# Splitting FFN weights: the last three bits as a byte in the sign word, the shift as an operation of its own

## The chip, the cores and the metric

The kernel runs on one core of one Trainium2 chip. The metric is the device time of one execution in microseconds, as the median of several runs. Lower is better.

## The reference

Attention with 32 global tokens and a local window, then a layer norm and a feed-forward block (FFN), all in float32. Cut to what matters:

```python
# q_l,k_l,v_l: (8, 8, 512, 64)   q_g,k_g,v_g: (8, 8, 32, 64)
out_g = softmax(scale * q_g @ k_all.T) @ v_all            # 32 global rows
s_ll  = where(|i - j| <= 32, scale * q_l @ k_l.T, -1e9)   # local band
out_l = softmax([scale * q_l @ k_g.T, s_ll]) @ [v_g, v_l]
x  = concat([out_g, out_l])       # (8, 576, 512) after heads are joined
xn = (x - mean(x)) / sqrt(var(x) + 1e-6) * g_ln
out = x + relu(xn @ w_ch1) @ w_ch2      # 512 -> 2048 -> 512
```

The two weight matrices, `w_ch1` (512 x 2048) and `w_ch2` (2048 x 512), come in as 64-bit floats.

## The kernel before, in words

**Chunks.** The 8 x 2 half sequences of local tokens are taken two at a time: eight chunks of 512 tokens, and a last chunk of the 256 global tokens. While TensorE does the FFN of one chunk, the attention of the next one runs beside it. The FFN loops over 16 blocks `f` of 128 hidden units. For each block TensorE makes `ph` (line 739: 12 matmuls, because each float is split into a high and a low part and three of the four products are kept), ScalarE writes its rectified high part `hh` (line 750), VectorE the low part `hl` (line 754), and TensorE adds 3 matmuls for each of four token tiles into `acc` (line 766).

**Weights.** A block of both matrices (128 partitions x 1024 elements) is loaded once as 64-bit words (`raw`, line 178) and turned into a high and a low 32-bit part that stay in on-chip memory for all chunks. The class `Weights` does that in steps, each one instruction on 128x1024 elements:

| step, token | line | engine | what it does |
|---|---|---|---|
| load, `wr` | 178 | SP queue | DMA of 1 MB into `raw` |
| head, `wa` | 183 | ScalarE | absolute value of the word with sign, exponent and high mantissa, scaled as a float to move the exponent, into `tmp` |
| tail, `wb` | 188 | ScalarE | makes the last three mantissa bits (0 to 7) from the upper half of the low word |
| bound, `wc` | 191 | VectorE | limits `tmp` to the largest float |
| join, `wd` | 195 | VectorE | shifts `tmp` left by 3 and ORs the three bits in |
| sign, `wg` | 201 | VectorE | ORs the sign in |
| high, `wh` | 208 | ScalarE | rounds to the high part `w[:, 0]` |
| low, `wl` | 212 | VectorE | `w[:, 1] = tmp - high` |

`tmp` has two buffers, so head of a block waits for low of the block two before it. All 16 blocks are split during the first chunk, between 17 and 125 us of the span.

**Order.** Every engine works in the order in which the program is written (`manual_schedule` covers all five). In the first chunk that order is the list of tokens `FIRST` (lines 50 to 71). Other tokens that matter here: `S`/`PS` scores on TensorE (lines 304, 428), `Rd`/`PRd` the reduction over scores on VectorE (321, 446), `Re`/`PRe` exponentials on ScalarE (335, 461), `C`/`PC` copies of turned probabilities (357, 481), `Na` the normalisation on VectorE (253), `Kt` transposes of normalised tokens on TensorE (667), `Kh` and `Kl` their high part on ScalarE (684) and low part on VectorE (688), `M`, `H`, `L`, `O` the four FFN steps of a block (739, 750, 754, 766), `X`/`PX` the attention output on VectorE (383, 519). A part of the list around joins 3 and 4:

```python
Kh1.0 wa4 Kl1.0 Kt1.1 wg3 PT0.1 Kh1.1 wb4 Kl1.1 wc4 Kt1.2 PC0.1 wd4 Kh1.2 Kt1.3 PV0 wh3
Kl1.2 Kh1.3 wl3 pv1 wr13 Kl1.3 wa5 wr14 PX0 Mb0 wr15 wb5 wg4 Mb1 Hb0 wc5 wh4 Lb0 PS1 wd5 Hb1
```

From the second chunk on the order comes from generators that hand out attention steps between the FFN's matmuls; among them are VectorE's 32x32 transposes (line 490) that the attention's second matmul (line 500) waits for.

Of the kernel before, what the change touches and what calls it, by code (L numbers as in the profile page):

```python
# [13 lines left out]
I32 = mybir.dt.int32  # L14
I16 = mybir.dt.int16
U16 = mybir.dt.uint16
BF16 = mybir.dt.bfloat16
I64 = mybir.dt.int64
AF = mybir.ActivationFunctionType
ALU = mybir.AluOpType  # L20
# [55 lines left out]

REBIAS = 2.0 ** -112
HUGE = 122877.9921875 * REBIAS
SIGN = -0x80000000


THIRD = 7.4999 / 65535

@with_exitstack
def attention_ffn_kernel(
# [11 lines left out]
    nc = tc.nc  # L97
# [71 lines left out]
    class Weights:  # L169
# [14 lines left out]

        def tail(self):
            third = self.raw.bitcast(U16).rearrange("p (n t) -> p n t", t=4)[:, :, 1]
            self.last = self.raw.bitcast(I32).rearrange("p (n t) -> p n t", t=2)[:, :, 0]
            nc.scalar.activation(self.last, third, AF.Copy, scale=THIRD)

        def bound(self):  # L190
            nc.vector.tensor_scalar(self.tmp, self.tmp, HUGE, None, ALU.min)

        def join(self):
            itmp = self.tmp.bitcast(I32)
            nc.vector.scalar_tensor_tensor(  # L195
                itmp, itmp, 3, self.last, ALU.logical_shift_left, ALU.bitwise_or
            )

        def sign(self):
            itmp = self.tmp.bitcast(I32)  # L200
            nc.vector.scalar_tensor_tensor(
                itmp, self.top, SIGN, itmp, ALU.bitwise_and, ALU.bitwise_or
            )

        def high(self):
# [910 lines left out]
```

## Time and profile before

| what | value |
|---|---|
| median of 3 runs | 937.46 us (937.17 to 938.05) |
| the profiled execution | 938.44 us, its span 936.7 us |
| mean granted TensorE clock in it | 0.989 |
| instructions | 21033 |

The span runs from the first to the last instruction of the profiled execution; the rest of that execution's time lies around it. The page gives busy time by engine, the span cut into 40 slices with busy tenths, the chain of work that ended last, and groups of instructions. Other views list waits (who waited for whom: total us, times, longest), the instructions of one tile (shortest, median and longest duration in ns, first and last start in us), a timeline (start, duration, engine, line; in brackets the idle time before it and what ended it), and busy time by stretch.

### The profile page before, as it was taken

The numbers are of one execution on the slowest core, as the hardware profiler recorded it, in microseconds if no ns is written. First come the engines' busy times: TensorE is split into PE (matmuls) and PEld (weight loads), VectorE is DVE, ScalarE is ACT, GpSimd is POOL, SyncE is SP. The second block draws the span as 40 slices with busy tenths as digits, with TensorE's granted clock in tenths as the row PEclk, the third lists the DMA queues.
The fourth block names the chain that finished last, engine by engine and source line by source line (L and its number), as shares of the span: only waits on it lengthen the run. The fifth ranks groups of instructions, "written<-read, shape, count | busy, mean of one in ns | idle before, by whom it ended". The sixth has DMA issues, their size and how long they took to land.

```text
span 936.7 us, 21033 instructions
## 1 busy us (share of the span) xinstructions
PE 911.1 (97%) x8652; PEld 722.4 (77%) x8652; DVE 572.0 (61%) x1852; ACT 313.4 (33%) x839; POOL 36.2 (4%) x121
## 2 busy tenths in 40 slices
PE   5899999999999999999999999999999999999997
PEld 3677777777778778777878778777877777777896
DVE  4999958765786657765776657765776623111311
ACT  5888733331323323231323323231422312211210
POOL 3000000000000000000000000000000000000000
PEclk9799999999999999999999999999999999999999
DMA  9993245212633263212533263213533151031100
GB/s 349 419 415 118 87 136 194 101 58 89 228 121 98 76 214 117 84 51 103 214 121 97 76 233 99 89 53 119 190 121 98 46 170 57 1 102 60 51 18 23
DMA packets 48880, 119.33 MB, mean 127 GB/s; under 512 B 5008, under 2 KB 16272, under 8 KB 45712
## 3 DMA queue, kind: packets, MB, share of 16 engines
q1 hardware_dynamic: 48784, 117.98, 35.4%
q8 instruction: 68, 1.11, 0.5%
q14 instruction: 28, 0.23, 0.1%
HBM read 100.14 MB, written 17.83 MB: 126 GB/s over the span
## 4 chain that ended last, share of the span: by engine, by line
PE 90%; DVE 2%; ACT 1%; issue 0%; DVEq 0%
PE acc L766 40%; PE ph L739 40%; PE sc L428 3%; PE pv L500 3%; PE t L667 1%; PE pv L620 1%; PE sc L566 1%; PE t L607 1%; DVE pt L490 1%; DVE w L212 0%; DVE tmp L195 0%; DVE ob L799 0%; ACT tmp L183 0%; ACT w L208 0%; DVE hl L754 0%
## 5 line engine op out<-in xcount | busy, mean ns | idle before, releaser
L766 PE MATMUL acc<-w,hh 128*128 128x512 f32 x1088 | 342.1, 396 | 0.0
L739 PE MATMUL ph<-xh,w 128*128 128x512 f32 (+1 forms) x1240 | 310.6, 377 | 0.2 <-DVE x L519 0.2
L754 DVE SCALAR_TENSOR_TENSOR hl<-ph,hh 128x512 fp32r<-128x512 f32 (+1 forms) x147 | 95.6, 651 | 279.0 <-ACT hh L750 278.6
L739 PEld LDWEIGHTS ph<-xh,w 128*128 128x128 f32 x1240 | 219.3, 189 | 47.4 <-issue 1.2
L750 ACT ACTIVATE hh<-ph 128x512 fp32r<-128x512 f32 (+1 forms) x147 | 83.1, 565 | 496.4 <-PE ph L739 496.3
L766 PEld LDWEIGHTS acc<-w,hh 128*128 128x128 f32 x1088 | 205.7, 189 | 45.7
L490 DVE STREAM_TRANSPOSE pt<-p 32x128 f32<-32x128 f32 x768 | 232.2, 302 | 11.1
L766 PE MATMUL acc<-w,hl 128*128 128x512 f32 x544 | 222.6, 409 | 0.3 <-DVE hl L754 0.2
L739 PE MATMUL ph<-xl,w 128*128 128x512 f32 (+1 forms) x524 | 143.8, 396 | 0.8 <-DVE xl L688 0.8
L766 PEld LDWEIGHTS acc<-w,hl 128*128 128x128 f32 x544 | 102.5, 188 | 26.5 <-issue 3.0
L739 PEld LDWEIGHTS ph<-xl,w 128*128 128x128 f32 x524 | 96.2, 189 | 26.2 <-issue 3.5
L461 ACT ACTIVATE p<-p,mn 128x128 f32<-128x128 f32 x224 | 87.2, 391 | 33.5 <-DVE mn L446 31.5
L446 DVE CUSTOM_DVE_ANT_0 p<-sc,mask 128x128 f32<-128x128 f32 x224 | 51.1, 285 | 0.1
L461 ACT ACTIVATION_READ_ACCUMULATOR p<-p,mn 128x1 f32 x224 | 42.0, 188 | 0.0
L500 PE MATMUL pv<-v,pt 128*32 128x64 f32 x1792 | 32.1, 222 | 2.3 <-DVE pt L490 2.3
L500 PEld LDWEIGHTS pv<-v,pt 128*32 128x32 f32 x1792 | 27.0, 111 | 8.9 <-issue 6.2
L428 PE MATMUL sc<-e 64*32 64x128 f32 x1792 | 32.4, 274 | 0.0
L428 PEld LDWEIGHTS sc<-e 64*32 64x32 f32 x1792 | 24.9, 105 | 9.5 <-issue 9.1
L242 ACT ACTIVATE x<-x,rs 128x512 f32<-128x512 f32 x30 | 22.8, 809 | 20.6 <-DVE rs L236 20.6
L688 DVE SCALAR_TENSOR_TENSOR xl<-t,g_sb,xh 128x512 fp32r<-128x512 f32 (+1 forms) x36 | 24.6, 689 | 7.9 <-ACT xh L684 7.7
L684 ACT ACTIVATE xh<-t,g_sb 128x512 fp32r<-128x512 f32 (+1 forms) x40 | 24.9, 624 | 12.0 <-PE t L667 11.8
L519 DVE TENSOR_TENSOR x<-pv,ri 128x256 f32<-128x256 f32 x56 | 21.2, 420 | 8.3 <-PE pv L500 5.7
(73 smaller groups left out, 477.0 us busy)
## 6 DMA issues: line engine op xcount, KB each, us to landing
v<-in_eu SPq DMA_DIRECT2D x28, 1024.0 KB, 7.1
e<-in_eu SPq DMA_DIRECT2D x28, 672.0 KB, 5.3
raw<-in_wd SPq DMA_DIRECT2D x16, 1024.0 KB, 12.7
gk<-in_gk SPq DMA_DIRECT2D x8, 1088.0 KB, 5.2
xs<-x SPq DMA_DIRECT2D x32, 256.0 KB, 7.1
ob<-xs SPq DMA_DIRECT2D x32, 256.0 KB, 7.3
out<-ob SPq DMA_DIRECT2D x32, 256.0 KB, 2.1
gv<-in_gv SPq DMA_DIRECT2D x16, 512.0 KB, 6.8
```

The source lines that it names most:

```text
L242: nc.scalar.activation(self.xn[:, j, :], self.x[:, j, :], AF.Identity, bias=self.rs[:, 1, j:j + 1], scale=self.rs[:, 0, j:j + 1],)
L428: nc.tensor.matmul(sc[h][gp, at:at + P], self.e[hd, j, w * WIN:(w + 1) * WIN], self.e[hd, j, k0 * WIN:(k0 + 4) * WIN], start=True, stop=Tr ...
L446: nc.vector.tensor_tensor_reduce(out=self.p[:, j, c], in0=self.sc[h][:, at:at + P], in1=masks[self.at[2], qb], scale=-QSCALE, scalar=BIG, ...
L461: nc.scalar.activation(self.p[:, j, c], self.p[:, j, c], AF.Exp, bias=self.mn[:, j, c:c + 1], scale=-1.0, accum_out=self.sm[:, j, c:c + 1],)
L490: nc.vector.transpose(out=self.pt[rp, j, :, gp], in_=self.p[gp, j, :, rp])
L500: nc.tensor.matmul(self.pv[gp, at:at + D], self.pt[:, j, 2 * h + qb, gp], self.v[:, j, 4 * qb + g, h * D:(h + 1) * D], start=True, stop=Tr ...
L684: nc.scalar.activation(hi, t[:, :n], AF.Copy, scale=g_sb[:, kt:kt + 1])
L688: nc.vector.scalar_tensor_tensor(lo, t[:, :n], g_sb[:, kt:kt + 1], f32(hi), ALU.mult, ALU.subtract)
L739: nc.tensor.matmul(ph[:, :n], w[:, kt, :], xx[kt][:, part.start:part.start + n], start=(i == 0), stop=(i == 3 * KT - 1),)
L750: nc.scalar.activation(hh[:, :n], self.ph[f, start][:, :n], AF.Relu)
L754: nc.vector.scalar_tensor_tensor(hl[:, :n], self.ph[f, start][:, :n], 0.0, f32(hh[:, :n]), ALU.max, ALU.subtract)
L766: nc.tensor.matmul(self.acc[t], a[:, ts], w, start=(f == 0 and i == 0), stop=(f == NF - 1 and i == 2),)
```

## The change

Tail writes its three bits no longer as a 32-bit number into the low word (whose content it had read), but as one byte into the lowest byte of the sign word, of which head has taken the absolute value before. Join then needs no second source: it is a shift by a constant, in place. Sign takes the sign bit and the three lowest bits of the sign word with one mask and ORs both in; it is still one instruction with two sources. The written order stays.

```diff
-SIGN = -0x80000000
+KEEP = -0x7FFFFFF9
...
         def tail(self):
             third = self.raw.bitcast(U16).rearrange("p (n t) -> p n t", t=4)[:, :, 1]
-            self.last = self.raw.bitcast(I32).rearrange("p (n t) -> p n t", t=2)[:, :, 0]
-            nc.scalar.activation(self.last, third, AF.Copy, scale=THIRD)
+            last = self.raw.bitcast(U8).rearrange("p (n t) -> p n t", t=8)[:, :, 4]
+            nc.scalar.activation(last, third, AF.Copy, scale=THIRD)
...
         def join(self):
             itmp = self.tmp.bitcast(I32)
-            nc.vector.scalar_tensor_tensor(
-                itmp, itmp, 3, self.last, ALU.logical_shift_left, ALU.bitwise_or
-            )
+            nc.vector.tensor_scalar(itmp, itmp, 3, None, ALU.logical_shift_left)
...
         def sign(self):
             itmp = self.tmp.bitcast(I32)
             nc.vector.scalar_tensor_tensor(
-                itmp, self.top, SIGN, itmp, ALU.bitwise_and, ALU.bitwise_or
+                itmp, self.top, KEEP, itmp, ALU.bitwise_and, ALU.bitwise_or
             )
```

More of the change, by code (lines that the diff above doesn't have):

```diff
@@ L16 @@
 U16 = mybir.dt.uint16
+U8 = mybir.dt.uint8
 BF16 = mybir.dt.bfloat16
```

## The prediction

> **What bounds the kernel now.** I read the page from the top: busy shares, the slices, then the chain that ended last.
>
> ```profile
> span 936.7 us, 21033 instructions
> PE 911.1 (97%) x8652; PEld 722.4 (77%) x8652; DVE 572.0 (61%) x1852; ACT 313.4 (33%) x839; POOL 36.2 (4%) x121
> PE   5899999999999999999999999999999999999997
> DVE  4999958765786657765776657765776623111311
> PE 90%; DVE 2%; ACT 1%; issue 0%; DVEq 0%
> ```
>
> TensorE (PE) is busy for 97% of the span and fills every slice after the first two or three (one slice is 23.4 us). VectorE (DVE) is full in slices 2 to 5, that is from about 23 to 117 us, where the weights are split. The change touches only that stretch, so the first question is where in it TensorE really waits. I asked for TensorE's waits from 58 us to the end:
>
> ```profile
> PE pv L500 <- DVE pt L490: 2.3, 3, 1.0
> PE ph L739 <- DVE x L519: 0.2, 1, 0.2
> ```
>
> Those are all: 0.2 us at the very start, and 2.3 us for the turned probabilities (L490), which come after the last weight. So from 58 us on nothing of the weight split holds TensorE up. A saving counts only if it brings TensorE's state at 58 us forward. The stretch before it, in columns PE, PEld, DVE, ACT, POOL, granted clock, DMA share and GB/s:
>
> ```profile
> 20.00:30.00 10.00, 6.12 (x168) 4.02 (x150) 8.16 (x40) 7.52 (x22) 0.82 (x2) 0.78 1.02 418
> 30.00:40.00 10.00, 7.81 (x89) 6.75 (x90) 9.58 (x20) 7.43 (x23) 1.59 (x4) 0.56 1.03 421
> 40.00:50.00 10.00, 9.62 (x142) 7.67 (x141) 9.83 (x32) 9.34 (x25) 1.29 (x3) 0.93 1.01 413
> 50.00:60.00 10.00, 8.03 (x111) 6.23 (x109) 9.78 (x16) 8.35 (x13) 0.35 (x1) 1.00 1.03 421
> ```
>
> Here VectorE is the fullest engine, TensorE has holes, and ScalarE (ACT) is close behind VectorE. That makes a VectorE saving look valuable. But two engines that take turns share a path, and the second one decides how much of the saving is left.
>
> **The change, part by part.** The weight steps, each x16 on 128x1024 elements:
>
> ```profile
> L191 DVE TENSOR_SCALAR tmp<-tmp x16: 679/690/697, 17.8 to 119.0; 128x1024 f32<-128x1024 f32 x16
> L195 DVE SCALAR_TENSOR_TENSOR tmp<-tmp,raw x16: 1209/1222/1255, 21.7 to 119.8; 128x1024 int32<-128x1024 int32 x16
> L201 DVE SCALAR_TENSOR_TENSOR tmp<-raw,tmp x16: 1214/1217/1236, 24.2 to 121.1; 128x1024 int32<-128x1024 int32 x16
> L183 ACT ACTIVATE tmp<-raw x16: 1109/1148/1319, 16.7 to 114.4; 128x1024 f32<-128x1024 f32 x16
> L188 ACT ACTIVATE raw<-raw x16: 1127/1150/1348, 17.7 to 115.6; 128x1024 int32<-128x1024 uint16 x16
> ```
>
> Join (L195) goes from two sources to one with a constant. The trace has no integer shift of that shape. From above it is bounded by itself, 1.222 us (no gain); from below by L191, 0.690 us, which has the same instruction kind, tile and element count and differs only in type and operation. I take L191: 1.222 - 0.690 = 0.532 us each, 16 x 0.532 = 8.5 us of VectorE time in all. [...]
>
> Tail (L188) stores a byte every 8 bytes instead of a word every 8 bytes. Its cost is bounded below by L183 at 1.148 us, which stores contiguous words at the same price (so here the scattered store costs nothing visible); above, no row has a byte store, and I take twice the row, 2.3 us, as the far end. I take 1.15 us, no change, because two very different store patterns already cost the same.
>
> Sign (L201) keeps its two sources; only the constant differs: 0. The wait on tail moves from join to sign, which stands one or more VectorE steps later in the written order, so no wait is added; no DMA and no queue position changes. Head must read the sign word before tail writes into it; both run on ScalarE in that order already. GpSimd is busy 0.35 to 1.59 us in 10, and L191 varies only from 679 to 697 ns beside it: 0 for contention.
>
> Of the 16 joins, five run before 58 us, so the ceiling is 5 x 0.532 = 2.66 us. Now each one, followed to what comes next (start, duration, idle and releaser):
>
> ```profile
> 21.65 1.22 DVE L195 SCALAR_TENSOR_TENSOR tmp<-tmp,raw 128x1024 int32<-128x1024 int32 x1
> 23.39 1.16 PE L304 MATMUL sc<-u 64*32 64x128 f32 x32 [2.68 <-DVE mn L321]
> 32.42 0.93 PE L667 MATMUL t<-ident,x 128*128 128x128 f32 x2 [0.70 <-DVE x L253]
> 33.96 1.22 DVE L195 SCALAR_TENSOR_TENSOR tmp<-tmp,raw 128x1024 int32<-128x1024 int32 x1
> 35.09 1.85 DVE L688 SCALAR_TENSOR_TENSOR xl<-t,g_sb,xh 128x256 fp32r<-128x256 f32 x4
> 35.93 0.49 ACT L684 ACTIVATE xh<-t,g_sb 128x256 fp32r<-128x256 f32 x1
> 39.21 1.22 DVE L195 SCALAR_TENSOR_TENSOR tmp<-tmp,raw 128x1024 int32<-128x1024 int32 x1
> 40.08 0.39 ACT L750 ACTIVATE hh<-ph 128x256 fp32r<-128x256 f32 x1 [1.10 <-PE ph L739]
> 40.49 0.42 DVE L754 SCALAR_TENSOR_TENSOR hl<-ph,hh 128x256 fp32r<-128x256 f32 x1
> 50.29 1.23 DVE L195 SCALAR_TENSOR_TENSOR tmp<-tmp,raw 128x1024 int32<-128x1024 int32 x1
> 54.13 1.23 DVE L195 SCALAR_TENSOR_TENSOR tmp<-tmp,raw 128x1024 int32<-128x1024 int32 x1
> 50.40 0.47 ACT L684 ACTIVATE xh<-t,g_sb 128x256 fp32r<-128x256 f32 x1 [0.35 <-PE t L667]
> 54.34 1.04 ACT L208 CAST w<-tmp 128x1024 fp32r<-128x1024 f32 x1
> 55.66 1.22 DVE L212 TENSOR_TENSOR w<-tmp,w 128x1024 fp32r<-128x1024 f32 x1
> 57.33 0.39 PE L739 MATMUL ph<-xl,w 128*128 128x256 f32 x1 [0.78 <-DVE xl L688]
> 58.37 0.71 PE L739 MATMUL ph<-xh,w 128*128 128x256 f32 x4 [0.19 <-DVE x L519]
> ```
>
> Join 0 (21.65): the next reduction on VectorE follows it, and TensorE's scores at 23.39 wait 2.68 us for that reduction. The whole 0.53 passes through: scores, the copies and exponentials behind them, up to the normalisation (L253) that releases the token transposes at 32.42. Shift there: -0.53.
>
> Join 1 (33.96): the four low halves L688 start behind it at 35.09 and end at 35.09 + 1.85 = 36.94. The fourth needs the fourth high half of ScalarE, which ends at 35.93 + 0.49 = 36.42, and 36.94 less a quarter of the 1.85 (0.46) is 36.48: it starts as that ends. That high half hangs on TensorE's transposes from 32.42, which are only 0.53 earlier. So this join's gain is lost; the shift stays -0.53.
>
> Join 2 (39.21): behind it is L754 at 40.49, which needs ScalarE's L750, ending 40.08 + 0.39 = 40.47, which had waited 1.10 us for TensorE. VectorE would only wait longer: lost, shift still -0.53.
>
> Joins 3 and 4 (50.29, 54.13): VectorE itself could be at -0.53 - 1.06 = -1.59 by 55.66. But L212 at 55.66 needs the cast L208, which ends at 54.34 + 1.04 = 55.38, and the ScalarE work from 50.40 to there has no pause over 0.15 us and starts from a transpose that is only 0.53 earlier. The cast ends at 55.38 - 0.53 = 54.85, L212 starts about 0.03 later, 54.88 in place of 55.66: -0.78. What was late before (VectorE) is not late now; ScalarE is late next, and 0.81 of the 1.06 goes into waiting for it. The steps behind it (L688, then L519), for which TensorE waits at 57.33 and 58.37, move by the same 0.78.
>
> Joins 5 to 15 lie beside TensorE work that never waits for them: 0, and 11 x 0.532 = 5.9 us of VectorE idle time. If that cover were gone (TensorE 2 us further ahead), part of it would count; 0.78 us is too little for that.
>
> Sum: -0.53 - 0 - 0 - 0.25 = -0.78 us. Against the profiled execution (938.44 us, of which 936.7 is its span and 1.7 lies around it) that is 937.7; the median of the runs, 937.46, is 1.0 below that execution, so there it is 936.7.
>
> One thing can move this sum, TensorE's clock, the seventh column:
>
> ```profile
> 38.03:41.44 3.41, 3.24 (x15) 2.87 (x15) 3.24 (x7) 2.31 (x9) 0.22 (x1) 0.50 1.02 423
> 157.50:160.91 3.41, 1.25 (x38) 0.76 (x38) 3.24 (x11) 0.00 (x0) 0.00 (x0) 1.00 0.98 377
> 160.91:164.32 3.41, 3.31 (x32) 2.67 (x33) 1.85 (x12) 1.80 (x9) 0.00 (x0) 0.50 1.09 373
> ```
>
> The clock is 0.50 up to 41.44, and again for one stretch of 3.41 us after a stretch in which TensorE was busy only 1.25. If those ends stay where they are while the work comes 0.78 us earlier, up to half of 0.78 is lost at each, so the gain shrinks to about 0.4; if they move with the work, it stays. One half-clock stretch more or less is worth up to 3.41 / 2 = 1.7 us. [...]
>
> **Rivals.** (a) VectorE's saving passes through in full, because ScalarE's and TensorE's small waits shrink too, or a half-clock stretch ends one step (1.7 us) sooner: -2.66, or -0.78 - 1.7 = -2.5, so about 934.9. For it: VectorE is 96 to 98% busy from 30 to 60 us. Against it: the ends 36.42, 40.47 and 55.38 above, each of another engine.
>
> (b) The shift doesn't reach the price of L191 and stays at the 1.22 us of L195: 0, so 937.4. Against it: same kind of instruction as L191.
>
> (c) Slower: the byte store. ScalarE's tails in question:
>
> ```profile
> 44.41 1.16 ACT L188 ACTIVATE raw<-raw 128x1024 int32<-128x1024 uint16 x1
> 52.39 1.15 ACT L188 ACTIVATE raw<-raw 128x1024 int32<-128x1024 uint16 x1
> 78.81 1.15 ACT L188 ACTIVATE raw<-raw 128x1024 int32<-128x1024 uint16 x1
> 80.89 1.18 ACT L188 ACTIVATE raw<-raw 128x1024 int32<-128x1024 uint16 x1
> 83.18 1.06 ACT L208 CAST w<-tmp 128x1024 fp32r<-128x1024 f32 x1 [0.64 <-DVE tmp L201]
> ```
>
> With x us more per tail, the one at 52.39 delays the cast at 54.34 by x: the sum becomes x - 0.81 (0.53 and the 0.28 between 55.38 and 55.66), and the one at 44.41 adds what exceeds the 0.35 us of idle time at 50.40. The two at 78.81 and 80.89 delay the cast at 83.18 by 2x - 0.64, which VectorE's savings there (two joins, 1.06) partly repay. At x = 1.15: 0.34 + 0.80 + 0.6 to 1.66, about +2.2 us, 939.7. The first two terms cancel at x = 0.58, so from a tail of about 1.7 us on the change loses; it exceeds 0.2% from x of about 1.1.
>
> **How the numbers follow.** A measurement of this kernel can tell about 0.2%, 1.9 us, from no change. Forecast as summed (-0.3 to -1.5): 0.56. (a): 0.2. (b): 0.12. (c): 0.12, of which 0.02 stays within 0.2%. Case (a) counts as faster, with 0.02 from the edge of the forecast: faster 0.22; slower 0.10; same 0.68. The likeliest is 936.7. The range takes in most of (a) and, above, (b) and the small end of (c): 935.0 to 938.4.
>
> **What the profile after would show.** Join at 0.69 us beside tail at 1.15 us, sign at 1.22. VectorE waiting for ScalarE's cast at L212 around 55 us, and for L750 around 40 us, where it hardly waited before. TensorE's last wait before its unbroken stretch (58.37) 0.5 to 1 us earlier, and VectorE's idle time between 58 and 124 us some 5 us larger with the span hardly changed. The prediction is wrong if join stays above 1.1 us, if tail exceeds 1.5 us, if that wait is more than 1.9 us earlier, or if the half-clock stretches before 41 us are fewer or more.

## The result, and the profile after

The change makes the kernel slower: 945.55 us (944.81 to 946.64, 4 executions) against 937.32 us (937.04 to 938.05, 4) of the kernel before, ratio 1.0083 (1.0066 to 1.0101), about 8 us. The profiled execution took 945.62 us.

From the page of the kernel after, the span, the busy shares, two rows of the slices and the chain by engine:

```profile
span 943.8 us, 21032 instructions
PE 913.6 (97%) x8652; PEld 723.9 (77%) x8652; DVE 564.7 (60%) x1852; ACT 332.3 (35%) x839; POOL 35.3 (4%) x121
PE   5888999999999999999999999999999999999997
ACT  5998964232332322232233323232323312211210
PE 88%; ACT 5%; DVE 3%; issue 1%; ACTq 0%; DVEq 0%
```

VectorE lost 7.3 us of work (572.0 to 564.7), as intended, but ScalarE gained 18.9 (313.4 to 332.3) and its share of the chain went from 1% to 5%. Two tile views of the kernel after, `raw` and `tmp` (shortest, median, longest ns):

```profile
L189 ACT ACTIVATE raw<-raw x16: 2474/2537/2605, 18.3 to 124.6; 128x1024 uint8<-128x1024 uint16 x16
```

```profile
L192 DVE TENSOR_SCALAR tmp<-tmp x16: 684/692/696, 18.3 to 126.6; 128x1024 f32<-128x1024 f32 x16
L196 DVE TENSOR_SCALAR tmp<-tmp x16: 682/686/695, 21.9 to 127.4; 128x1024 int32<-128x1024 int32 x16
L200 DVE SCALAR_TENSOR_TENSOR tmp<-raw,tmp x16: 1214/1220/1311, 23.9 to 128.1; 128x1024 int32<-128x1024 int32 x16
```

Join (L196) does the shift at 0.686 us, the price of the float pass beside it, and sign (L200) is unchanged. Tail (L189) went from 1.150 to 2.537 us, 1.39 more. ScalarE's next instruction starts before a tail has ended, so a tail holds the engine for less than that: 1.04 us before (78.81 to 79.85) and 2.24 after (82.62 to 84.86), 1.2 more each. Sixteen times that is 19 us, the 18.9 above.

TensorE's waits from 58 us to the end (us in total, times, longest), kernel after:

```profile
PE acc L765 <- DVE hl L753: 4.5, 3, 2.9
PE pv L499 <- DVE pt L489: 2.3, 3, 1.0
```

The second line stood there before; the first is new. Beside the weight split TensorE waited for nothing from 58.37 us on; it now waits for the low part of a block's activations. The fixed 70 us in which most weights are split, kernel before and then kernel after (columns PE, PEld, DVE, ACT, POOL, granted clock, DMA share, GB/s):

```profile
60.00:130.00 70.00, 69.94 (x614) 56.40 (x614) 61.70 (x117) 53.24 (x100) 2.68 (x5) 1.00 0.37 138
```

```profile
60.00:130.00 70.00, 66.36 (x596) 53.35 (x595) 54.59 (x114) 64.37 (x97) 1.77 (x4) 0.98 0.38 138
80.00:90.00 10.00, 9.39 (x45) 7.47 (x44) 6.70 (x9) 9.93 (x9) 0.00 (x0) 1.00 0.00 0
90.00:100.00 10.00, 7.05 (x143) 5.40 (x143) 9.41 (x29) 9.16 (x10) 1.15 (x2) 0.84 0.55 169
96.74:100.15 3.41, 3.41 (x9) 2.63 (x9) 3.36 (x19) 3.38 (x5) 1.29 (x2) 0.50 0.61 181
```

ScalarE and VectorE have changed places as the fuller engine. From 80 to 90 us ScalarE has no gap, VectorE idles, and from 90 to 100 TensorE is down to 7.05 us of work. Then comes a half-clock stretch (96.74 to 100.15) where the kernel before had full clock.

What VectorE waits for from 58 to 140 us, kernel after, is ScalarE each time. The first three rows (activations, head, cast) make 15.8 us, where the same three made 5.8 before; the last is sign waiting for a tail, once, the wait that moved there from join:

```profile
DVE hl L753 <- ACT hh L749: 5.9, 7, 1.5
DVE tmp L192 <- ACT tmp L184: 5.4, 6, 1.7
DVE w L211 <- ACT w L207: 4.5, 6, 1.6
DVE tmp L200 <- ACT raw L189: 0.5, 1, 0.5
```

The same instruction of TensorE, followed in both kernels, dates the loss (start, duration, idle and releaser). Before:

```profile
61.06 0.50 PE L766 MATMUL acc<-w,hl 128*128 128x512 f32 x1
89.63 0.50 PE L766 MATMUL acc<-w,hl 128*128 128x512 f32 x1
124.36 0.39 PE L766 MATMUL acc<-w,hl 128*128 128x512 f32 x1
158.44 0.30 PE L500 MATMUL pv<-v,pt 128*32 128x64 f32 x2 [0.29 <-DVE pt L490]
```

After, with the steps that lead to two of them:

```profile
53.19 2.47 ACT L189 ACTIVATE raw<-raw 128x1024 uint8<-128x1024 uint16 x1
56.14 0.69 PE L666 MATMUL t<-ident,x 128*128 128x128 f32 x2 [1.84 <-ACT pt L480]
56.34 1.04 ACT L207 CAST w<-tmp 128x1024 fp32r<-128x1024 f32 x1
57.42 1.23 DVE L211 TENSOR_TENSOR w<-tmp,w 128x1024 fp32r<-128x1024 f32 x1 [0.45 <-ACT w L207]
59.86 2.60 ACT L189 ACTIVATE raw<-raw 128x1024 uint8<-128x1024 uint16 x1
63.18 0.50 PE L765 MATMUL acc<-w,hl 128*128 128x512 f32 x1
81.18 1.05 ACT L207 CAST w<-tmp 128x1024 fp32r<-128x1024 f32 x1
82.62 2.52 ACT L189 ACTIVATE raw<-raw 128x1024 uint8<-128x1024 uint16 x1
86.06 2.56 ACT L189 ACTIVATE raw<-raw 128x1024 uint8<-128x1024 uint16 x1
88.95 1.04 ACT L207 CAST w<-tmp 128x1024 fp32r<-128x1024 f32 x1
95.51 0.50 PE L765 MATMUL acc<-w,hl 128*128 128x512 f32 x1 [2.94 <-DVE hl L753]
132.90 0.50 PE L765 MATMUL acc<-w,hl 128*128 128x512 f32 x1 [0.93 <-DVE hl L753]
167.08 0.30 PE L499 MATMUL pv<-v,pt 128*32 128x64 f32 x2 [0.29 <-DVE pt L489]
```

- 61.06 to 63.18: 2.1 us late. At 42 us the two executions were still 0.1 us apart (a cast at 42.08 before, at 42.16 after). The tail at 53.19 starts 0.8 later than before and holds ScalarE 1.2 longer, so the cast behind it moves from 54.34 to 56.34, the low part behind that from 55.66 to 57.42, and the next tail (59.86) is longer again. TensorE is held up beside it: its transpose at 56.14 waits 1.84 us for a ScalarE copy behind the same tail, and its clock then stands at 0.50 from 55.77 to 59.19, where the kernel before had full clock. Both paths reach 63.18 within 0.1 us of each other.
- 89.63 to 95.51: 5.9 late. ScalarE comes to the two tails at 82.62 and 86.06 already 3.8 late (the cast at 81.18 stood at 77.36 before). They add 2.0, so that the next cast starts at 88.95 (83.18 before); its low part (`w[:, 1]`) and the activations queue behind it, and TensorE waits 2.94 us. An earlier wait of 0.6 us makes up most of the rest.
- 124.36 to 132.90: 8.5 late, 2.7 more than at 95.51. Another wait took 0.93 of that; the other 1.7 stands with the half-clock stretch that follows the hole of 2.94, in which three matmuls of L765 take 1.28 us (97.24 to 98.52) where they took 0.70 just before it (95.85 to 96.55).
- 158.44 to 167.08: 8.6 late. Of this the span keeps 7.1 (943.8 less 936.7). Most of the difference is the half-clock stretch that the kernel before had just behind that point (160.91 to 164.32, worth up to half of its 3.41 us, 1.7); the kernel after has none there.

### The profile page after: what moved, and what is told of

It reads as the page before. It is cut to its first block, busy times and chain, and to the rows that moved or that the text cites. A ratio compares the mean times of both kernels' runs of the same rounds, so it can differ in the third digit from the quotient of the medians.

```text
span 943.8 us, 21032 instructions
## 1 busy us (share of the span) xinstructions
PE 913.6 (97%) x8652; PEld 723.9 (77%) x8652; DVE 564.7 (60%) x1852; ACT 332.3 (35%) x839; POOL 35.3 (4%) x121
## 4 chain that ended last, share of the span: by engine, by line
PE 88%; ACT 5%; DVE 3%; issue 1%; ACTq 0%; DVEq 0%
PE acc L765 39%; PE ph L738 38%; PE pv L499 3%; PE sc L427 3%; ACT raw L189 2%; PE t L666 2%; PE pv L619 1%; ACT tmp L184 1%; PE sc L565 1%; DVE w L211 1%; PE t L606 1%; DVE pt L489 1%; ACT p L460 0%; ACT w L207 0%; DVE hl L753 0%
## 5 line engine op out<-in xcount | busy, mean ns | idle before, releaser
L765 PE MATMUL acc<-w,hh 128*128 128x512 f32 x1088 | 343.3, 397 | 0.0
L765 PEld LDWEIGHTS acc<-w,hh 128*128 128x128 f32 x1088 | 206.2, 190 | 45.7
L765 PE MATMUL acc<-w,hl 128*128 128x512 f32 x544 | 222.9, 410 | 5.1 <-DVE hl L753 5.0
L765 PEld LDWEIGHTS acc<-w,hl 128*128 128x128 f32 x544 | 102.7, 189 | 32.1 <-DVE hl L753 6.4
L189 ACT ACTIVATE raw<-raw 128x1024 uint8<-128x1024 uint16 x16 | 40.4, 2540 | 0.3
```

Source lines behind the costliest of these rows:

```text
L189: nc.scalar.activation(last, third, AF.Copy, scale=THIRD)
L765: nc.tensor.matmul(self.acc[t], a[:, ts], w, start=(f == 0 and i == 0), stop=(f == NF - 1 and i == 2),)
```

## Experiments

**Is it the byte, or any store narrower than a word?** `two_bytes` writes the same value as two bytes.

```diff
-last = self.raw.bitcast(U8).rearrange("p (n t) -> p n t", t=8)[:, :, 4]
+last = self.raw.bitcast(U16).rearrange("p (n t) -> p n t", t=4)[:, :, 2]
```

> The changed kernel, but tail stores two bytes (the lower half of the sign word) instead of one; sign masks the rest away, so the computation is complete. Theory A (the store of single bytes made tail 2.54 us, and ScalarE's extra 16 x 1.39 = 22 us is the whole loss): tail back at 1.15 us, join at 0.69, time 936.7 (937.3 less 0.5 to 1.0). Theory B (any store narrower than a word is slow): tail near 2.5 us, time near 945.5. Theory C (the loss comes from the wait on tail that moved to sign, or from join's faster mode): tail 1.15 us and yet a time over 941.

Its tail in the tile view:

```profile
L189 ACT ACTIVATE raw<-raw x16: 2469/2552/2682, 17.1 to 120.3; 128x1024 uint16<-128x1024 uint16 x16
```

945.08 us (942.85 to 945.39), ratio 1.0082 (1.0070 to 1.0095). Two bytes cost the same as one, in the instruction and in the kernel: it isn't a matter of one-byte stores.

**The shift without the byte store.** `word_tail` keeps the old tail and the new join.

```diff
+KEEP = -0x80000000
...
+last = self.raw.bitcast(I32).rearrange("p (n t) -> p n t", t=2)[:, :, 0]
```

> The new join alone: tail as before (a word into the low word), join a shift by a constant, sign masks the sign bit alone, so the three last bits are left out. Theory A: the shift is worth what the prediction's sum says, 936.5 (-0.4 to -1.2 against before). Theory C: slower than before by some us. If the prediction's following of the waits was wrong and the saving passes through: 934.7.

935.82 us (933.68 to 938.1), ratio 0.9983 (0.9972 to 0.9994): 0.6 to 2.6 us faster than before, 1.6 in the middle. Tail 1.157, join 0.687. So everything that the change loses comes with the narrow store. The shift by itself is a gain; its interval holds the 0.78 that had been summed and, near its end, the 2.5 of rival (a), so the time alone doesn't tell those two apart.

**Does the step matter?** `bytes_dense` writes the bytes side by side. The mask of `word_tail` stands in it too, as in `no_tail`, `half_words`, `bytes_every_4` and `other_source`: these kernels leave out the last three bits, and this one loses the signs of 128 columns besides.

```diff
+last = self.raw.bitcast(U8)[:, :KT * P + DM]
```

> Tail stores its 1024 bytes next to each other instead of one in every eight (over the first 128 pairs of words, so the signs of 128 columns are lost and the three last bits are left out). If the scatter of the bytes is what costs: tail 1.1 to 1.2 us and a time near 936.7. If it is the element of one byte itself: tail 2.5 us and a time near 945.5.

```profile
L189 ACT ACTIVATE raw<-raw x16: 1117/1154/1264, 17.4 to 112.8; 128x1024 uint8<-128x1024 uint16 x16
```

The same type, element count and conversion as the slow tail, at less than half its time; 935.83 us in its one execution. The type isn't the price: it is the narrow element together with its step.

**Is it ScalarE's time alone?** `before_twice` is the kernel before with its word tail issued twice. The second tail reads the word that the first has just overwritten, so it writes zeros and the last three bits are left out; nothing else differs.

> The kernel before with tail done twice (two word stores, 2 x 1.04 us from start to start on ScalarE), join and sign as before. It adds 16 x 1.04 = 16.6 us to ScalarE without any byte store. Theory A (ScalarE's time is the mechanism): about three quarters of the loss and more, since join keeps its 1.22 us: 943 to 946. Theory C: about 937 to 938.

946.71 us (946.46 to 947.98), ratio 1.0105 (1.0092 to 1.0118). TensorE's waits, 0 to 200 us, one row:

```profile
PE acc L767 <- DVE hl L755: 4.6, 5, 2.5
```

In the same stretch the kernel after has 5.0 us of this wait. ScalarE's busy time rises from 313.4 to 330.6 us, by 17.2, in ordinary word stores, where the change added 18.9. The loss is 9.8 us (1.05% of the 937.12 us of before beside it), here without the faster join. Nothing peculiar to the byte's place is needed; occupying ScalarE is enough.

**Give the tail to an idle engine.** `pool_tail` issues it on GpSimd.

```diff
-nc.scalar.activation(last, third, AF.Copy, scale=THIRD)
+nc.gpsimd.tensor_scalar(last, third, THIRD, None, ALU.mult)
```

> The changed kernel with tail, byte store and all, on GpSimd instead of ScalarE; the written order of the steps stays. GpSimd is idle for most of the stretch, so a tail of up to some 4 us fits in time (16 blocks in 108 us). Theory A (the loss is ScalarE's time): the loss is gone, and ScalarE is rid of 16 x 1.04 us besides; 935.8 as with the new join alone, down to 933. Theory D (the loss hangs on the bytes being stored late or on sign's wait for them, whoever stores them): 940 or more. If GpSimd's tail takes over 5 us, or holds up the reciprocal sums and the power behind it on GpSimd, also 940 or more, and the trace would show it in those waits.

957.78 us (954.96 to 959.56), ratio 1.0212 (1.0191 to 1.0234). Two tile views, with the tail and with the join:

```profile
L189 POOL TENSOR_SCALAR raw<-raw x16: 4289/4642/5436, 17.7 to 135.4; 128x1024 uint8<-128x1024 uint16 x16
```

```profile
L196 DVE TENSOR_SCALAR tmp<-tmp x16: 677/1516/2993, 21.1 to 140.8; 128x1024 int32<-128x1024 int32 x16
```

GpSimd takes 4.64 us for it, more than the 4 that were taken to fit, and VectorE's join beside it stretches from 0.686 to a median of 1.516 us. That lengthens VectorE's work as well (588.3 us busy, 564.7 in the kernel after), so the run says nothing on what a ScalarE freed of the tail is worth.

**No tail at all.** `no_tail` leaves the instruction out.

> The new join with no tail at all (the three last bits are left out): ScalarE is rid of 16 x 1.04 = 16.6 us. It shows whether ScalarE is late next in the stretch before 58 us, as the prediction said. If it is: joins 3 and 4 give up to 0.8 us more than with the word tail, 935.0 against 935.8 or lower. If not: the same 935.8.

934.66 us (933.52 to 937.5), ratio 0.9968 (0.9953 to 0.9984), about 3 us. The interval overlaps that of `word_tail`, which shares the new join, so the traces have to tell the two apart. TensorE's wait at 58.37 before, in the first and then in the second:

```profile
55.90 0.71 PE L738 MATMUL ph<-xh,w 128*128 128x256 f32 x4 [0.17 <-DVE x L518]
```

```profile
57.10 0.73 PE L737 MATMUL ph<-xh,w 128*128 128x256 f32 x4 [0.19 <-DVE x L517]
```

These starts alone can't be compared, since the two executions left the first phase differently. But the high part of ScalarE that stood at 50.40 before stands at 48.24 and at 49.77 here, so between the two points `word_tail` gains -2.47 less -2.16, 0.31 us, and `no_tail` -1.27 less -0.63, 0.64. With the tail out of the way, joins 3 and 4 bring twice as much, 0.33 us more where up to 0.8 was expected. It is one execution of each, but the way fits: ScalarE was late there.

**Where does the loss arise?** `late_bytes` uses word tails for the first five blocks, whose last three bits it leaves out, and byte tails for the other eleven.

```diff
+if self.f < 5:
+    last = self.raw.bitcast(I32).rearrange("p (n t) -> p n t", t=2)[:, :, 0]
+else:
+    last = self.raw.bitcast(U8).rearrange("p (n t) -> p n t", t=8)[:, :, 4]
...
+itmp, self.top, KEEP if self.f >= 5 else -0x80000000, itmp, ALU.bitwise_and, ALU.bitwise_or
```

> Byte store and full mask from block 5 on only; blocks 0 to 4 store words as before and leave the three last bits out. All 16 blocks have the new join. Blocks 0 to 4 are the ones whose tails run before 58 us. If the loss comes about in that stretch (as rival (c) of the prediction priced its first terms): under 938. If it builds up beside TensorE's unbroken stretch, where I had called the cover good for 2 us: 936 + 5 to 7 = 941 to 943, with TensorE waiting for the low halves of the hidden units (hl) around 84, 95 and 132 us.

943.56 us (940.54 to 944.5), ratio 1.0060 (1.0044 to 1.0077), about 5.6 us. Three rows of TensorE's timeline:

```profile
81.08 0.50 PE L768 MATMUL acc<-w,hl 128*128 128x512 f32 x1 [0.64 <-DVE hl L756]
92.42 0.79 PE L768 MATMUL acc<-w,hl 128*128 128x512 f32 x1 [2.92 <-DVE hl L756]
129.49 0.50 PE L768 MATMUL acc<-w,hl 128*128 128x512 f32 x1 [0.90 <-DVE hl L756]
```

The three waits of the kernel after (0.6, 2.94, 0.93) are all here, 3 us earlier. Most of the loss comes from the tails after 58 us, beside TensorE's stretch without holes.

**Which widths and steps?** `half_words` and `bytes_every_4` write two bytes and one byte every 4 bytes. Other than the two expectations say, no sign is lost: the stores miss the byte that holds it.

```diff
+last = self.raw.bitcast(U16)[:, :2 * (KT * P + DM)].rearrange("p (n t) -> p n t", t=2)[:, :, 0]
...
+last = self.raw.bitcast(U8)[:, :4 * (KT * P + DM)].rearrange("p (n t) -> p n t", t=4)[:, :, 0]
```

> Tail stores two bytes in every four (over the first half of the raw words, so signs of columns are lost and the three last bits are left out). The dense byte store took 1.15 us, two bytes in every eight 2.55 us, a word in every eight 1.15 us. If the cost is that a word is only partly written: 2.5 us again. If it is the step of eight bytes together with a narrow element: 1.15 to 1.3 us.

> Tail stores one byte in every four (over the first half of the raw words; signs of columns are lost, the three last bits are left out). So far a tail took 1.15 us for dense bytes, 1.38 us for two bytes in four, 2.55 us for one or two bytes in eight. If the step sets the price: about 1.4 us. If the share of the stored span that is left untouched sets it (three quarters here as with two in eight): about 2.5 us.

Tail of `half_words`, then of `bytes_every_4`:

```profile
L189 ACT ACTIVATE raw<-raw x16: 1347/1382/1402, 17.5 to 113.3; 128x1024 uint16<-128x1024 uint16 x16
```

```profile
L189 ACT ACTIVATE raw<-raw x16: 1340/1379/1409, 17.4 to 113.2; 128x1024 uint8<-128x1024 uint16 x16
```

936.11 and 936.02 us in one execution each. Half a word in every word costs 1.38 us, between the two prices that were expected, so an incomplete word alone isn't what doubles the time; the same element with its step doubled to 8 bytes costs 2.55. One byte and two cost the same at either step.

**Store or source?** `other_source` makes the same byte store from another tile, with float elements.

> Tail stores one byte in every eight as in the changed kernel, but reads another tile (the identity, dense float32), so the bytes hold no bits of the weights and the sign mask leaves them out. If the slow tail comes from reading and writing the same eight bytes: 1.05 to 1.15 us. If it is the store alone: 2.5 us.

```profile
L189 ACT ACTIVATE raw<-ident x16: 2477/2536/2606, 17.3 to 123.2; 128x1024 uint8<-128x1024 f32 x16
```

2.536 us, and 945.78 us in its one execution: another source costs the same, so the price is that of the store.

**The same store on VectorE.** `vector_tail` issues the tail there, with all else as after.

> Tail with its byte store on VectorE instead of ScalarE, all else as changed. ScalarE is rid of 16 x 1.04 us, VectorE gets one tail more per block for the 0.53 us that the join saves. If VectorE's byte store costs one pass of about 0.7 to 1.2 us: VectorE +0.2 to 0.7 us per block against before, 5 blocks before 58 us, 936 to 940. If it is as slow as ScalarE's (2.5 us): VectorE +2.0 us per block, 948 or more.

```profile
L189 DVE TENSOR_SCALAR raw<-raw x16: 1282/1325/1353, 18.0 to 124.8; 128x1024 uint8<-128x1024 uint16 x16
```

1.325 us, half of ScalarE's price, but 946.02 us in its one execution, between the two ranges that were expected: VectorE, relieved by 0.536 us in join, gets 1.325 back, 0.8 us more per block in all.

**The change in one block only.** `first_only` has the new tail, join and sign in block 0 and the old ones in the other fifteen.

> The kernel before with the change in block 0 alone (byte store, shift by a constant, full mask), complete in what it computes. Its tail runs where ScalarE then idles for 2.35 us, its join is the one whose whole saving I had passed through. By the prediction's steps: -0.5 us, below what a measurement tells, so within 0.2% of before. If block 0's join were worth nothing: 0; if the whole gain of the new join came from it and grew on the way: -1.6.

937.89 us (934.2 to 938.94), ratio 1.0001 (0.9988 to 1.0013). The half-clock stretches of its profiled execution:

```profile
17.00:30.43 13.43, 7.57 (x242) 5.20 (x241) 11.90 (x49) 12.74 (x33) 1.95 (x5) 1.00 1.02 417
30.43:33.84 3.41, 2.80 (x42) 2.37 (x40) 3.31 (x8) 2.76 (x6) 0.00 (x0) 0.50 1.01 407
33.84:44.00 10.16, 7.99 (x146) 6.61 (x138) 9.93 (x23) 8.74 (x24) 0.22 (x1) 1.00 1.03 421
```

No difference is measured; the interval (-1.1 to +1.2 us) holds the 0.53 that join 0 should bring and holds zero as well. That term stays open. The rows say why it is hard to see: this execution had one half-clock stretch of 3.41 us between 17 and 44 us and took 934.2 us, while the kernel before in its profile had five, the last one ending at 41.44.

## Why the prediction was wrong

It forecast 936.7 us, within 0.2% of before; the kernel is 0.8% slower and above the range.

**The step that failed** is the term of the tail: "I take 1.15 us, no change, because two very different store patterns already cost the same." Both patterns were of whole words, dense and every 8 bytes, and neither had a narrow element. The far end named for it, 2.3 us, was short of the 2.537 measured. The sign of being wrong that was named for it, a tail above 1.5, came true. A row that doesn't contain the new property can't be the near one.

**Rival (c) was the mechanism**, with a chance of 0.12 and a price that was too small. At x = 1.39 its terms give 0.58 + 1.04 = 1.6 at the low part behind the cast at 54.34; the trace has 57.42 less 55.66, 1.8. The third, 2x - 0.64 = 2.1 less up to 1.06, gives 1.1 to 2.1, in all 2.7 to 3.8; the trace has 5.9 by that point and 8.5 by 124 us. (With the 1.2 us for which a tail really holds ScalarE, (c) gives less still.) Four things were missed. The tails between those it listed count too: ScalarE is 3.8 late before the pair of tails begins. The repayment by two joins doesn't come, since ScalarE, not VectorE, is now late. The later tails of blocks 10 to 15 count as well (the wait of 0.93). And the hole of 2.94 us is followed by a half-clock stretch, with which 1.7 us of the loss stand; that is in part luck, as said below. The cover for joins 5 to 15 ("beside TensorE work that never waits for them") was true for taking time from VectorE; the sum never examined it for adding time to ScalarE, and rival (c) did so at one place only. ScalarE had 70.00 - 53.24 = 16.8 us idle there, enough in sum for 11 x 1.39 = 15.3, but the written order puts two tails ahead of a cast that the next low parts need, and the idle time stands elsewhere.

**Join** was right: 0.690 forecast, 0.686 measured; sign was right at 1.22, but it did get a wait for the tail, once, 0.5 us.

**Following the waits** was right where `word_tail`, in which only the join is new, can show it. The forecast was that joins 1 and 2 are lost to a wait for ScalarE's high halves and that L212 then waits for the cast. Its timeline, and the high part used above:

```profile
30.26 0.93 PE L666 MATMUL t<-ident,x 128*128 128x128 f32 x2 [0.89 <-DVE x L252]
34.30 0.48 DVE L687 SCALAR_TENSOR_TENSOR xl<-t,g_sb,xh 128x256 fp32r<-128x256 f32 x1 [0.37 <-ACT xh L683]
38.33 0.42 DVE L753 SCALAR_TENSOR_TENSOR hl<-ph,hh 128x256 fp32r<-128x256 f32 x1 [0.60 <-ACT hh L749]
48.24 0.47 ACT L683 ACTIVATE xh<-t,g_sb 128x256 fp32r<-128x256 f32 x1
53.18 1.23 DVE L211 TENSOR_TENSOR w<-tmp,w 128x1024 fp32r<-128x1024 f32 x1 [0.45 <-ACT w L207]
```

The three waits are there, 0.37, 0.60 and 0.45 us. The shift against before is -2.16 at the transposes (30.26 for 32.42) and still -2.16 at 48.24 (for 50.40): nothing is seen of joins 1 and 2. (Between the two points `word_tail` stood at half clock for 0.6 us longer than the kernel before, which can hide up to 0.3.) Joins 3 and 4 bring 0.31, where 0.25 was forecast. Whether join 0 brings 0.53 can't be read from the -2.16: with the same new join `no_tail` reaches the transposes at 31.79, 0.63 earlier than the profile of before, and the kernel after at 32.51, 0.09 later; and the execution profiled before was itself 1.0 above its median. The measured 0.6 to 2.6 us holds the forecast 0.78, but its middle is twice that, so the size of the whole gain stays open.

**The clock** moves more than it was allowed for. After a hole of 2.94 us came a stretch of 3.41 us at half clock (96.74 to 100.15), deep in the kernel; and the half-clock stretches between 17 and 44 us differ in number and place between executions: five in the profile of before, six in that of the kernel after, four in `word_tail`, one in `first_only`. Within one execution their starts lie whole steps of 3.41 us apart: 55.77 and 96.74 in the kernel after (12 steps), 17.55 and 160.91 before (42). Counted in such steps, the kernel after has its hole in one, with TensorE busy for 1.23 us from 93.33 to 96.74. What followed differed with how a hole lay: the three waits for the turned probabilities, 2.3 us in all in both profiles, left TensorE busy for 1.25 us in one step before (157.50 to 160.91), and half clock followed; in the kernel after they lie across two steps, and at full clock it went on:

```profile
165.01:168.42 3.41, 2.14 (x102) 1.62 (x102) 3.20 (x11) 0.00 (x0) 0.00 (x0) 1.00 0.95 312
168.42:171.83 3.41, 2.42 (x35) 1.90 (x36) 2.94 (x15) 1.69 (x9) 0.00 (x0) 1.00 1.05 356
171.83:175.25 3.42, 3.42 (x17) 2.74 (x16) 2.89 (x14) 2.10 (x9) 0.23 (x1) 1.00 1.04 396
```

`two_bytes`, too, had a wait of 3.0 us for the low part, but its mean granted clock was 0.991 where the kernel after had 0.985, and this execution, at 942.85 us, was the shortest of its six. The prediction's own sum for the clock has a slip as well: half lost at each of two ends would leave 0.2 of the 0.78, not 0.4.

**What stays open** is why a narrow element every 8 bytes costs 2.5 us on ScalarE and every 4 bytes 1.38, whether join 0's 0.53 arrives in the end, and what the shift is worth without the narrow store, beyond 0.6 to 2.6 us.

## What to carry to other kernels

A change of an operand's width or step can be a change of price (here from 1.15 to 2.54 us), and a row with another width doesn't bound it: look for a row with the same element and step, or take the far end seriously. Before moving work, ask of each engine touched what an added microsecond would do where TensorE doesn't wait now; cover against a saving on one engine is no cover against a cost on another. Idle time in sum says nothing when the order is written out: look at the steps between the last free moment and the next thing that TensorE needs.

## What the hardware showed beside this

In these runs ScalarE's price for 1024 elements per partition goes by the width and step of what it writes: a word every 8 bytes 1.15 us, dense bytes 1.15, one or two bytes every 4 bytes 1.38, one or two bytes every 8 bytes 2.54 to 2.55. A byte and a word, each every 8 bytes, differ by 1.39 us.

With the tail on GpSimd (4.64 us) some of VectorE's passes took longer: one join 2.99 us and one bound 2.75, where the longest of the kernel after took 0.70 each. The runs show that they grew, not by what.
